# Two blocks of the last output, one early product, and rows of x turned a unit sooner

## The chip, the cores and the metric

The kernel runs on one core of a Trainium2 chip. A core has a matrix engine (TensorE, PE in the profile), a vector engine (VectorE, DVE), a scalar engine (ScalarE, ACT), GpSimd (POOL) and SyncE (SP), which in this kernel only issues DMAs. ACT and POOL issue DMAs too, each in order with its other work. All engines run their own instruction streams and wait for one another through semaphores. The metric is the device time of one execution in microseconds; three runs of the kernel before gave a median of 887.59 us (887.34 to 888.34).

## What is computed

Two blocks one after the other, in float32, for 4 sequences of 768 rows. The first is attention with 8 heads of 64 columns, in which a query sees only the keys that fall to the same of 16 centroids; the second is a normalization with a two-layer network and a residual.

```python
q_assign = argmax(q_n @ c_n.T); k_assign = argmax(k_n @ c_n.T)
scores = where(q_assign == k_assign, q @ k.T / sqrt(64), -1e9)
x = softmax(scores) @ v                      # (4, 768, 512) when the heads are put side by side
xn = (x - mean(x)) / sqrt(var(x) + 1e-6) * g_ln
out = x + relu(xn @ w_ch1) @ w_ch2           # w_ch1 (512, 2048), w_ch2 (2048, 512)
```

## The kernel before

**Attention.** The 32 heads are worked on as 16 pairs, numbered 0 to 15, one pair after another; pair 13, for instance, is the second of sequence 3. For each pair PE makes the masked scores (`scores`, L401), ACT the exponentials (L396), PE the weighted values (`weigh`, L413), and DVE adds the exponentials up over the keys (`add_up`, L431), of which there are two halves, g = 0 and 1. `finish` (L457) has four parts: the denominators and their way through DRAM (0, 1), the multiply of the numerators by the reciprocals on DVE with the store of the result, `xT_d`, by SP (2, L506 and L507), and, for the first two sequences, the rows of x (3). For pair 13 part 3 does nothing but forget the tile. In the last pair the sums of each half are five additions of 128x768 (L438).

**The network, with fewer products.** A matrix product of two by two blocks is made with seven products instead of eight (the parts 1, 2, 6, 5, 7, 4, 3 of `first_layer`, L897), and sums of blocks are made ahead by DVE (`x_sum`, `w1_sums`). The first layer runs over eight units, j = 0 to 7 (`first_units`, L1335), each with seven such products: part 1 starts a PSUM bank and ACT copies it out as `p1` (L881), then later parts add to the same bank. For sequence 0 the second layer does the same (`second_layer`, L990). For sequences 1 to 3 the second layer is a *deep layer* (`deep_layer`, L1224): each of the seven products, in the order 4, 7, 1, 6, 5, 2, 3, is itself made with seven (the steps (m, way), L1019 to L1029). The last steps are (3, 1), (3, 2), (2, 4), (2, 3), (3, 6), (3, 5), (3, 7), (3, 4), (3, 3). Each is eight matmul instructions of 128x192, for which `deep_product` (L1134) takes weights from a ring of ten buffers that SP fills (`ring_load`, L1080), and DVE or ACT then moves the bank to SBUF with sums (L1157 to L1180). Steps 1, 6, 7, 4 of one m add to one bank, so that (3, 4) can start only when DVE has read the bank after (3, 7), into `u`.

**Rows of x.** Sequences 2 and 3 need x by rows for their statistics, while attention left it by columns in `xT_d`. Eight blocks have to be turned: a load (`columns_load`, L530), a DVE transpose, and four stores (`rows_out`, L516). Five of them are turned during sequence 0's second layer. The other three are turned during sequence 1's first layer, at the ends of units (`unit_end`, L1440): loaded at the ends of units 0, 2 and 4, turned at the ends of 1, 3 and 5, and their stores issued by SP at the beginning of the next unit's end (`leave`, L1448). At the end of unit 6 come the statistics of the next sequence (L608, L611) and four ring loads. The tiles come from the tag `row` of two buffers, which the two rows of statistics use too.

**The end.** In sequence 3's deep layer the right half of the output comes in quarters of 192 rows and 128 columns, each after its last step: (3, 2), (3, 7), (3, 4) and (3, 3). `last_part` (L1237) has DVE transpose a quarter in blocks of 32x32 (L1247) and stores it with four DMAs of 24 KB in runs of 128 bytes (L1251), dealt to the queues of SP, ACT and POOL.

**What sets the order.** In most of the kernel the order of the instructions on PE, DVE, ACT and SP is that of the program text (`manual_schedule`). In sequence 0's second layer that holds for PE and DVE alone, and a planner places the DMAs of SP and ACT. SP holds a DMA until the buffer it writes is free, and what is behind it waits.

Of the kernel before, what the change touches and what calls it, by code (L numbers as in the profile page):

```python
# [23 lines left out]
def kernel(  # L24
# [701 lines left out]
    with tc.manual_schedule(engines=order | {mybir.EngineType.Pool}):  # L726
        def extras(n, at):
            for job in extra.pop((n, at), ()):
                job()

        def turn_pair(n):
            for side in (1, 0):
                prep_transpose(n, side)
                load(n + 1, "qk"[side])

        def weight(n, part):
            begun = convert.get((n - 1, 1)) if part == 0 and n - 1 in BEGIN else None
            m = convert.get((n, part))
            if begun is not None:
                weight_end(begun)  # L740
            if m is not None:
                split_weight(m)
                if (part, n in BEGIN) != (1, True):
                    weight_end(m)

        def weight_end(m):
            join_weight(m)
            load_weight(m + 2)

        for n in range(len(pairs)):  # L750
            nxt = n + 1 < len(pairs)
            own = range(2 * NT * n, 2 * NT * (n + 1))
            if n == 0:
                turn_pair(1)
            elif nxt:
                prep_route(n + 1)
            load(n + 1, "v")
            for i in own:
                if i >= AHEAD:
                    scores(i)  # L760
                if n == 0 and i + 1 == NT:
                    prep_sims(1)
                    prep_route(1)
            extras(n, "scores")
            if 1 < n and nxt:
                finish(n - 2, 1)
            if n and n + 2 < len(pairs):
                turn_pair(n + 2)
            if not nxt:
                finish(n - 1, 1)  # L770
            add_up(n, 0)
            extras(n, "sums")
            if not nxt:
                finish(n - 2, 2)
                finish(n - 2, 3)
            if n and nxt:
                finish(n - 1, 0)
            if nxt:
                for piece in pieces[:4]:
                    prep_mask(n + 1, *piece)  # L780
            add_up(n, 1)
            if n == 0:
                turn_pair(2)
            for i in own[:NT]:
                weigh(i)
            if nxt:
                for piece in pieces[4:]:
                    prep_mask(n + 1, *piece)
            weight(n, 0)
            if n > 1 and nxt:  # L790
                finish(n - 2, 2)
                finish(n - 2, 3)
            extras(n, "weigh")
            for i in own[NT:]:
                weigh(i)
            if n + 2 < len(pairs):
                prep_sims(n + 2)
            elif nxt:
                finish(n, 0)
            weight(n, 1)  # L800
            extras(n, "end")
            if n + 2 == len(pairs):
                finish(n - 1, 1)
            if not nxt:
                for part in (2, 3):
                    finish(n - 1, part)
# [327 lines left out]
    def deep_product(st, m, way):  # L1134
        p = st[m]
        if way == 1:
            p["x"] = ps("x_ps")
        if way == 2:
            p["y"] = ps("y_ps")
        if way == 5:  # L1140
            p["z"] = ps("z_ps")
        name = {2: "y", 5: "z", 3: "z"}.get(way, "x")
        bank = p[name][:, :QC]
        w, a = ring["at"].pop((m, way)), st["q", m][way]
        for c in range(NQH):
            nc.tensor.matmul(  # L1146
                bank, w[:, c, :], a[:, c],
                start=way in (1, 2, 5) and c == 0, stop=c == NQH - 1, skip_group_check=True,
            )

        def part(t, r, j):
            return None if t is None else t[:, j].rearrange("p (t a r) -> p t a r", a=2, r=Q)[:, :, r]

        def rows_of(t):
            return t.rearrange("p (t r) -> p t r", r=Q)

        def put_in(o, x, of=bank):  # L1157
            if x is None:
                nc.scalar.copy(o, rows_of(of))
            else:  # L1160
                nc.vector.tensor_tensor(o, rows_of(of), x, ALU.add)  # L1161

        def kept_sum(key, r, j):
            t = p[key] = rows_of(hid.tile([P, HC], F32, tag="p", name=key, bufs=5)[:, :QC])
            put_in(t, part(p["add"], r, j))

        if way == 1:
            kept_sum("p1", 0, 0)
        elif way == 2:
            put_in(part(p["to"], 0, 0), p["p1"])  # L1170
        elif way == 6:
            kept_sum("u2", 0, 1)
        elif way == 7:
            kept_sum("u3", 1, 1)
        elif way == 4:
            put_in(part(p["to"], 1, 0), part(p["add"], 1, 0))
        elif way == 3:
            put_in(part(p["to"], 0, 1), p["u2"])
        if way == 7:
            put_in(part(p["to"], 1, 1), p["u3"], p["z"][:, :QC])  # L1180

# [42 lines left out]
    def deep_layer(b, more, st):  # L1224
# [3 lines left out]
        def ahead_of(m):  # L1228
            p = st[m] = {}
            onto = {2: 1, 3: 5}.get(m)  # L1230
            p["add"] = done.get(onto)
            p["to"] = done[m] = done[onto] if onto else unit(f"m{m}")

        def sum_onto(i, j):
            nc.vector.tensor_tensor(done[i], done[i], done[j], ALU.add)

        def last_part(o, way):  # L1237

            part = {2: (0, 0), 7: (1, 1), 4: (1, 0), 3: (0, 1)}.get(way)
            if part is None:  # L1240
                return
            r, j = part
            queues = {
                7: (nc.sync, nc.scalar, nc.gpsimd, nc.sync), 4: (nc.scalar, nc.gpsimd, nc.sync, nc.scalar),
            }.get(way, (nc.sync, nc.scalar))
            y = unit("y_end")[:, 0, :QC]
            nc.vector.transpose(y, o[:, j].rearrange("p (t a r) -> p t a r", a=2, r=Q)[:, :, r])  # L1247
            to = out[b].rearrange("(a r t) m -> a (r t) m", r=Q, t=NT)[r]
            for i in range(P // Q):
                m = MH + j * P + i * Q  # L1250
                queues[i % len(queues)].dma_start(  # L1251
                    out=to[:, m : m + Q], in_=y[i * Q : (i + 1) * Q].rearrange("r (t f) -> r t f", f=Q)
                )
# [35 lines left out]
        if more:  # L1289
# [8 lines left out]
            jobs[2, 3] = [rest(0, 0, 2), lambda: rest_load(b, 1)]  # L1298
            jobs[3, 6] = [lambda: x_sum(b + 1, 1)]
            jobs[3, 5] = [lambda: w1_sums(b + 1, 0, (0, 1))]  # L1300
            jobs[3, 4] = [lambda: x_sum(b + 1, 2)]
            later(
                rest(1, 1, 7), out_of(1, 1, 7), out_of(0, 0, 2), None,
# [68 lines left out]
    with tc.manual_schedule(engines={mybir.EngineType.PE, mybir.EngineType.DVE}):  # L1372
# [6 lines left out]
        norm_load(1)  # L1379
        rows_load(1, 0)  # L1380

        def column():
            return early.tile([P, S], F32, tag="col", name="col", bufs=2)

# [10 lines left out]
        def do(f, *args):  # L1395
            return lambda: f(*args)
# [24 lines left out]
            (7, 2): [turn_columns, do(norm_apply, 1, 1, 0), w2_whole],  # L1421
            (4, 0): [do(norm_apply, 1, 1, 1), do(norm_apply, 1, 1, 2)],
            (4, 1): [turn_columns, do(norm_apply, 1, 1, 3)],
            (4, 2): [do(x_sum, 1, 1), do(x_sum, 1, 2)],
            (3, 0): [do(x_sum, 1, 3)],
            (3, 1): [do(x_sum, 1, 4), do(w1_sums, 1, 0)],
            (3, 2): [],
# [7 lines left out]
    with tc.manual_schedule(engines=order | {mybir.EngineType.SP}):  # L1435
# [4 lines left out]
        def unit_end(b, j):  # L1440
# [29 lines left out]
                norm_stat_rows(b + 1)  # L1470
            leave(4)
            if b == 1:
                def row():
                    return xpool.tile([P, S], F32, tag="row", name="col", bufs=2)

                if turning and j % 2:
                    columns_turn(row, lambda out, in_: leaving.append((out, in_)))
                elif asked and j % 2 == 0:
                    columns_load(row)
            if j > 4:  # L1480
                for _ in range(4):
# [3 lines left out]
        for b in range(1, B):  # L1485
            deep[b] = {}
            if b + 1 < B:
                rows_load(b + 1, 0)
            if b == 1:
                outer["t"] = w2_back(1)  # L1490
                first_units(b, 0)
            else:
                first_layer(b, 0, 1)
                first_layer(b, 0, 2)
                first_layer(b, 0, 6)
                relu(1)
                w1_sums(b, 0, (2, 3))
                x_sum(b, 3)
                first_layer(b, 0, 5)
                first_layer(b, 0, 7)  # L1500
                x_sum(b, 4)
                w1_sums(b, 1)
            unit_end(b, 0)
            for j in range(1, NFH):
                first_units(b, j)
                unit_end(b, j)
            relu(len(summed))
            inner_sums(deep[b], ORDER[0], cs=slice(NQH - 1, NQH))
            if b == 1:
                first.close()  # L1510
                units = pool("units", 1)
            deep_layer(b, b + 1 < B, deep[b])
# [232 lines left out]
```

## Time and profile before

| | us |
|---|---|
| median of three runs | 887.59 (887.34 to 888.34) |
| the profiled execution | 888.41 |
| its span, from the first instruction to the last | 886.6 |
| PE busy | 871.5 (98%) |
| DVE busy | 704.6 (79%) |
| ACT busy | 402.7 (45%) |
| granted clock of PE, mean | 0.997 |

The span is 1.8 us shorter than the execution that holds it. Busy times are sums over instructions of an engine, overlaps counted once. In the lines that follow, a timeline row gives the start in us, the time to the end of the last of its instructions in us, engine, source line, operation, the tiles out and in, and the count; in brackets stands the idle time of the engine before it and what ended it. A row of waits gives who waited for what, the total in us, how many times, and the longest. SPq and ACTq are the queues of SP and ACT, whose rows are the times that issuing took.

### The profile page before, as it was taken

To read this page: it belongs to the slowest core of one execution; us is meant where nothing else is said; L and a number is where in the kernel's file an instruction comes from. 1 tells how busy PE (TensorE), PEld (TensorE's weight loads), DVE (VectorE), ACT (ScalarE), POOL (GpSimd) and SP (SyncE) were. 2 spreads that over 40 slices of the span, in tenths; PEclk is the share of its full clock that TensorE was granted. 3 is DMA by queue.
4 is the path that set the end of the run, shared out by engine and by line. 5 is a ranking of instruction groups with operands and counts; after the bars stand their busy time and mean duration, and the time that the engine had idled before them with its cause. 6 is when DMAs were issued, how large, how long until landed. Compare 5 with 4: busy or idle time off the path is not lost.

```text
span 886.6 us, 13193 instructions
## 1 busy us (share of the span) xinstructions
PE 871.5 (98%) x4644; PEld 575.0 (65%) x4644; DVE 704.6 (79%) x1149; ACT 402.7 (45%) x739; POOL 77.8 (9%) x143
## 2 busy tenths in 40 slices
PE   8999999999999999999999999999999999999995
PEld 5444444444444445568885558996557997557995
DVE  6899999999999878959577787997556896646774
ACT  6777788888898823330004552103552101333110
POOL 1012121212222212110000000000000000000000
PEclk9999999999999999999999999999999999999998
DMA  7777899999886337876675878854236862511875
GB/s 159 134 131 129 150 173 186 209 203 190 184 197 172 97 117 202 235 197 215 186 175 183 261 239 293 299 155 98 57 71 204 284 190 54 110 62 37 275 201 98
DMA packets 251642, 151.01 MB, mean 170 GB/s; under 512 B 193696, under 2 KB 209200, under 8 KB 250544
## 3 DMA queue, kind: packets, MB, share of 16 engines
q1 hardware_dynamic: 219824, 130.75, 56.0%
q0 software_dynamic: 7776, 15.03, 8.7%
q10 hardware_dynamic: 23968, 4.30, 2.7%
q8 instruction: 39, 0.64, 0.3%
q14 instruction: 35, 0.29, 0.1%
HBM read 108.40 MB, written 33.25 MB: 160 GB/s over the span
## 4 chain that ended last, share of the span: by engine, by line
PE 93%; DMA 2%; DVE 2%; issue 1%; SPq 1%; ACT 1%; POOL 0%; DVEq 0%; ACTq 0%; POOLq 0%
PE x_ps L855 19%; PE s_ps L401 16%; PE a_ps L413 12%; PE x_ps L1146 12%; PE z_ps L855 9%; PE z_ps L1146 6%; PE x_ps L963 5%; PE y_ps L855 5%; PE y_ps L1146 3%; PE z_ps L963 2%; PE sim_ps L320 1%; PE den_ps L469 1%; PE y_ps L963 1%; DVE es L438 1%; DMA flat<-dsb 1%
## 5 line engine op out<-in xcount | busy, mean ns | idle before, releaser
L401 PE MATMUL s_ps<-t,t 64*128 64x384 f32 x768 | 154.8, 483 | 0.0
L401 PEld LDWEIGHTS s_ps<-t,t 64*128 64x128 f32 x768 | 67.9, 187 | 39.0 <-issue 38.3
L1146 PE MATMUL x_ps<-lower,w 128*128 128x192 f32 x448 | 81.0, 327 | 1.9 <-DMA w<-w_d 1.0
L886 DVE TENSOR_TENSOR lower<-z_ps,u 128x384 f32<-128x384 f32 x56 | 31.1, 555 | 60.1 <-PE z_ps L855 48.9
L1146 PEld LDWEIGHTS x_ps<-lower,w 128*128 128x128 f32 x448 | 74.0, 190 | 4.0 <-DVE u L1161 1.5
L396 ACT ACTIVATE e<-s_ps 128x768 f32<-128x768 f32 x84 | 67.1, 812 | 7.0 <-PE s_ps L401 6.4
L396 ACT ACTIVATE w<-s_ps 128x768 f32<-128x768 f32 x80 | 64.5, 813 | 8.3 <-PE s_ps L401 7.7
L401 PE MATMUL s_ps<-mask,mask 64*128 64x384 bf16 x384 | 62.7, 323 | 1.0 <-ACT e L396 0.6
L894 ACT ACTIVATE lower<-lower 128x384 f32<-128x384 f32 x88 | 45.0, 522 | 37.7 <-DVE lower L886 37.7
L881 ACT COPY u<-x_ps 128x384 f32<-128x384 f32 x64 | 30.7, 479 | 68.3 <-PE x_ps L855 68.3
L413 PE MATMUL a_ps<-e,v_sb 128*64 128x384 f32 x336 | 57.6, 488 | 0.0
L881 ACT COPY p<-x_ps 128x384 f32<-128x384 f32 x32 | 15.1, 471 | 91.4 <-PE x_ps L855 88.7
L413 PE MATMUL a_ps<-w,v_sb 128*64 128x384 f32 x320 | 55.2, 488 | 0.0
L855 PE MATMUL x_ps<-xt,ws 128*128 128x384 f32 x128 | 46.6, 487 | 0.9 <-ACT p L881 0.9
L855 PE MATMUL x_ps<-xn,ws 128*128 128x384 f32 x128 | 46.6, 487 | 0.0
L855 PE MATMUL x_ps<-xn,w 128*128 128x384 f32 x128 | 46.6, 487 | 0.0
L855 PE MATMUL z_ps<-xt,ws 128*128 128x384 f32 x128 | 46.5, 486 | 0.0
L855 PE MATMUL y_ps<-xn,w 128*128 128x384 f32 x128 | 46.5, 486 | 0.0
L855 PE MATMUL x_ps<-xt,w 128*128 128x384 f32 x128 | 46.5, 486 | 0.0
L855 PE MATMUL z_ps<-xn,ws 128*128 128x384 f32 x128 | 46.5, 486 | 0.0
L413 PEld LDWEIGHTS a_ps<-e,v_sb 128*64 128x64 f32 x336 | 23.5, 137 | 31.8 <-issue 28.7
L1251 POOL DMA_DIRECT2D out_dram<-y_end x2 | 1.2, 584 | 489.7 <-DMA out_dram<-y 488.6
(226 smaller groups left out, 1677.9 us busy)
## 6 DMA issues: line engine op xcount, KB each, us to landing
w<-w_d SPq DMA_DIRECT2D x84, 256.0 KB, 3.5
raw<-in_moe_w_ch_dram SPq DMA_DIRECT2D x32, 512.0 KB, 4.9
w<-w_t SPq DMA_DIRECT2D x36, 256.0 KB, 5.3
w<-tb POOLq DMA_DIRECT2D x32, 256.0 KB, 5.5
w_d<-wt SPq DMA_DIRECT2D x7, 1024.0 KB, 5.5
w<-w_all SPq DMA_DIRECT2D x27, 256.0 KB, 3.1
v_sb<-in_v_dram SPq DMA_DIRECT2D x32, 192.0 KB, 4.3
xr<-x_d SPq DMA_DIRECT2D x24, 256.0 KB, 2.8
```

The lines of the kernel that those rows point to most:

```text
L320: nc.tensor.matmul(sim[r : r + Q, :HC], cT[:, pr, :, :].rearrange("p j c -> p (j c)"), prepared[n][side][:, g * HC : (g + 1) * HC], start= ...
L396: nc.scalar.activation(e, s[:, :, :HC], AF.Exp, scale=SCALE)
L401: nc.tensor.matmul(s[:, j, :HC], of_keys[:, keys], of_queries[:, o : o + HC], start=part == first, stop=part != first, skip_group_check=True,)
L413: nc.tensor.matmul(acc[j * D : (j + 1) * D, :HC], loaded[n]["v"][:, j, c, :], e[:, j, :], start=(c == 0), stop=(c == NT - 1),)
L438: nc.vector.tensor_tensor(es, e[0] if m == 1 else es, e[m], ALU.add)
L469: nc.tensor.matmul(den[r : r + Q, :HC], ones, sums[n, g][h][:, j, :], start=h == 0, stop=h == parts - 1, tile_position=(0, r), skip_group_ ...
L855: nc.tensor.matmul(bank[:, :HC], lhs[:, c, :], rhs[:, c], start=first and c == 0, stop=c == NDH - 1, skip_group_check=True,)
L881: nc.scalar.copy(t, bank[:, :HC])
L886: nc.vector.tensor_tensor(h, bank[:, :HC], other, ALU.add)
L894: nc.scalar.activation(h, h, AF.Relu)
L963: nc.tensor.matmul(bank[:, :MH].rearrange("p (h f) -> p h f", h=2), hidden[lhs + (c,)][:, tt * P : (tt + 1) * P], rhs[:, :, c], start=firs ...
L1146: nc.tensor.matmul(bank, w[:, c, :], a[:, c], start=way in (1, 2, 5) and c == 0, stop=c == NQH - 1, skip_group_check=True,)
```

## The change

Four things are edited.

1. In the last pair of the attention, parts 2 and 3 of `finish` for pair 13 are called after `add_up(15, 1)` instead of before it.
2. In the deep layers of sequences 1 and 2, the first product of the next sequence's first layer is made after step (3, 7), in front of (3, 4); it no longer opens the next sequence.
3. The sixth block of x is loaded during sequence 0's second layer, after product (4, 2), and the three turns stand at the ends of units 0, 2 and 4 instead of 1, 3 and 5; the loads stand at the ends of 1 and 3.
4. The last two quarters of the output, (3, 4) and (3, 3), are summed into a tile of their own with the rows in order, turned by PE in two halves of 96 rows, copied out of PSUM by DVE and ACT, and stored with one DMA each by SP and ACT, in runs of 512 bytes. Of the quarter (3, 7), the fourth store goes to POOL instead of SP.

```diff
@@ in the loop over the pairs
             extras(n, "sums")
-            if not nxt:
-                finish(n - 2, 2)
-                finish(n - 2, 3)
...
             add_up(n, 1)
+            if not nxt:
+                finish(n - 2, 2)
+                finish(n - 2, 3)
@@ in deep_product
-        elif way == 4:
-            put_in(part(p["to"], 1, 0), part(p["add"], 1, 0))
-        elif way == 3:
-            put_in(part(p["to"], 0, 1), p["u2"])
+        elif way in (4, 3):
+            r, j = (1, 0) if way == 4 else (0, 1)
+            to = part(p["to"], r, j)
+            if "ends" in p:
+                p["ends"][way] = unit("end")[:, 0, :QC]
+                to = p["ends"][way].rearrange("p (r t) -> p t r", r=Q)
+            put_in(to, part(p["add"], 1, 0) if way == 4 else p["u2"])
@@ in deep_layer
+            if m == ORDER[-1] and not more:
+                p["ends"] = {}
...
-            queues = {
-                7: (nc.sync, nc.scalar, nc.gpsimd, nc.sync), 4: (nc.scalar, nc.gpsimd, nc.sync, nc.scalar),
-            }.get(way, (nc.sync, nc.scalar))
+            queues = (nc.sync, nc.scalar, nc.gpsimd, nc.gpsimd) if way == 7 else (nc.sync, nc.scalar)
+            if way in (4, 3):
+
+                columns = st[ORDER[-1]]["ends"][way]
+                turned, y = ps("turned"), unit("y_end")
+                n = QC // 2
+                for i in range(2):
+                    nc.tensor.transpose(
+                        turned[:n, i * P : (i + 1) * P], columns[:, i * n : (i + 1) * n], ident
+                    )
+                    copy = (nc.vector.tensor_copy, nc.scalar.copy)[i]
+                    copy(y[:n, i, :P], turned[:n, i * P : (i + 1) * P])
+                    (nc.sync, nc.scalar)[i].dma_start(
+                        out=out[b, r * QC + i * n : r * QC + (i + 1) * n, MH + j * P : MH + (j + 1) * P],
+                        in_=y[:n, i, :P],
+                    )
+                return
...
             jobs[3, 5] = [lambda: w1_sums(b + 1, 0, (0, 1))]
+            jobs[3, 7] = [lambda: first_layer(b + 1, 0, 1)]
             jobs[3, 4] = [lambda: x_sum(b + 1, 2)]
@@ in sequence 0's second layer
-            (4, 2): [do(x_sum, 1, 1), do(x_sum, 1, 2)],
+            (4, 2): [do(x_sum, 1, 1), do(x_sum, 1, 2), do(columns_load, row)],
@@ in unit_end
-                if turning and j % 2:
+                if turning and j % 2 == 0:
                     columns_turn(row, lambda out, in_: leaving.append((out, in_)))
-                elif asked and j % 2 == 0:
+                elif asked and j % 2:
                     columns_load(row)
@@ at the start of sequences 2 and 3
-                first_layer(b, 0, 1)
                 first_layer(b, 0, 2)
```

More of the change, by code (lines that the diff above doesn't have):

```diff
@@ L1380, with row @@
         rows_load(1, 0)
+        def row():
+            return xpool.tile([P, S], F32, tag="row", name="col", bufs=2)
         def column():
@@ L1472, in unit_end @@
             if b == 1:
-                def row():
-                    return xpool.tile([P, S], F32, tag="row", name="col", bufs=2)
-                if turning and j % 2:
+                if turning and j % 2 == 0:
                     columns_turn(row, lambda out, in_: leaving.append((out, in_)))
-                elif asked and j % 2 == 0:
+                elif asked and j % 2:
                     columns_load(row)
```

## The prediction

> **What bounds the kernel now.** I read the page, then TensorE's (PE's) waits, then the timelines around each wait and at the end.
>
> ```profile
> span 886.6 us, 13193 instructions
> ...
> PE 871.5 (98%) x4644; PEld 575.0 (65%) x4644; DVE 704.6 (79%) x1149; ACT 402.7 (45%) x739; POOL 77.8 (9%) x143
> ```
>
> PE is the bound: no edit here takes products away, so only what lies outside its 871.5 us can be won, 15.1 us in all. Its waits (total, times, longest) name places that the diff touches:
>
> ```profile
> PE x_ps L1146 <- DVE u L1161: 1.4, 3, 0.5
> ...
> PE x_ps L1146 <- DMA w<-w_d: 1.0, 1, 1.0
> PE x_ps L855 <- ACT p L881: 0.9, 1, 0.9
> ```
>
> The first is three stalls, one in each deep layer between products (3, 7) and (3, 4). The timeline of PE shows what such a stall costs:
>
> ```profile
> 599.65 1.46 PE L1146 MATMUL x_ps<-lower,w 128*128 128x192 f32 x8
> 601.57 1.57 PE L1146 MATMUL x_ps<-lower,w 128*128 128x192 f32 x8 [0.45 <-DVE u L1161]
> ```
>
> The gap is 0.45. In the chain of waits a product that follows another without a gap adds 1.30, but this one adds 1.57: a stall also costs a restart of 0.27, so 0.7 each.
>
> **A: the multiply of pair 13 behind the last key sums.** The stall at 322.65 waits for ACT's copy of `p`, and that for DVE's sums `es`, in order behind the multiply of L506:
>
> ```profile
> 317.14 0.95 DVE L645 TENSOR_TENSOR xn<-xn 128x768 f32<-128x768 f32 x1
> 318.01 0.95 DVE L506 TENSOR_TENSOR rb<-x,rb 128x768 f32<-128x768 f32 x1
> 318.88 0.95 DVE L438 TENSOR_TENSOR es<-e 128x768 f32<-128x768 f32 x1
> ```
>
> ```profile
> 322.11 0.48 ACT L881 COPY p<-x_ps 128x384 f32<-128x384 f32 x1 [2.64 <-DVE es L438]
> ```
>
> Moved, its slot (318.88 - 318.01 = 0.87) comes free: the copy ends at 321.72 instead of 322.59. The product before is done at 321.70, so a gap of about 0.07 and the restart stay. **Gain 0.87**; most, the gap, 0.94, with the restart, 0.27: 1.2. Least 0, if the copy meets another wait. What is late now: the multiply itself (to about 323.2) and its one 384 KB store on SP, from 318.99 to about 324.2, just ahead of pair 14's store at 324.98. Only a column load much later reads it. DVE's total up to 324.0 is the same, so pair 14's multiply and the first hidden sum behind it (324.87) do not move. From 322.7 to 543.8 PE is busy 221.1 of 221.1 us, with no other wait to swallow the gain.
>
> **B: one product of the next sequence between (3, 7) and (3, 4).** It happens twice (sequences 2 and 3). The product moved takes 1.29 (chain of waits); DVE's `u` is ready 0.45 after (3, 7) ends, so the product covers it. **Gain 2 x 0.7 = 1.4**; the third stall stays. The operands are there: its rows' last scaling is in step (5, 5), its set of sums in (3, 5). What becomes tight: the step's ACT copy of 0.48 is issued earlier on an ACT that had idled 18.6 us; the moved product no longer separates (3, 3) from the next two. The second sum of x, which product 6 needs, ended at 604.40 and product 6 began at 606.85; it now begins 0.7 sooner and the sum ends about 0.6 later (1.29 - 0.7), so 1.1 us of room is left. Product 7's sum (done 609.21, used 609.43) has only 0.2, but both ends hang on product 2's end, which moves with them. Bounds: 0 (another wait takes the place) to 1.42.
>
> **C: rows of x turned one unit sooner.** A turn is one DVE transpose (0.94 to 0.98) and, a unit later, four stores of 96 KB on SP; its load is one 384 KB DMA on SP. Of the three turns left, the last one's stores now stand in front of the statistics and the next weights:
>
> ```profile
> 526.30 6.50 SPq L1216 DMA_DIRECT2D x_d<-col  x4
> 532.90 1.58 SPq L1064 DMA_DIRECT2D w_d<-wt  x1
> 534.58 0.46 SPq L608 DMA_DIRECT2D stat_d<-st  x1
> 538.94 0.86 SPq L611 DMA_DIRECT2D stat_row<-stat_d  x2
> 539.85 0.42 SPq L1088 DMA_DIRECT2D w<-w_d  x1
> ```
>
> ```profile
> 544.84 2.84 PE L1146 MATMUL x_ps<-lower,w 128*128 128x192 f32 x16 [0.99 <-DMA w<-w_d]
> ```
>
> PE's weights issued at 539.85 landed after 4.86 (chain of waits), 0.99 late. With the stores a unit earlier (about 513 to 520, where SP waited 8.4 for DVE), `w_d` goes when DVE's last difference is done, at 532.34 or up to 0.94 sooner. I keep 4.36 from the statistics' store to the load and 0.91 from there to the weights, and take 0.37 (its usual issue) for 1.58: weights at 532.4 + 0.4 + 4.36 + 0.9 = 538.1 at the latest, 1.75 sooner where 0.99 is needed. **Gain 0.99 + 0.24** (2.84 against 2 x 1.30) **= 1.23**; least 0, if the landing is slower by more than 0.76. The costs: 0.97 of DVE in the first unit, which was busy 6.62 of 9.10 us there; the w1 sums behind it would end at 482.6, and the product that reads them starts at 485.5, so it hides. The other turns move into units with 6.8 and 6.5 of about 9. On SP the stores now precede that unit's weight stores; their readers follow two units later.
>
> **D: the tail.** Before, the last two quarters go through a DVE transpose (0.38), then four stores each:
>
> ```profile
> 878.31 0.38 DVE L1247 STREAM_TRANSPOSE y_end<-m 128x192 f32<-128x192 f32 x1
> ```
>
> ```profile
> 879.97 1.25 ACTq L1251 DMA_DIRECT2D out_dram<-y_end  x2
> 880.42 0.57 SPq L1251 DMA_DIRECT2D out_dram<-y_end  x1
> ```
>
> The data are ready at 878.69, but the queues are not: SP's last issue ends at 880.99 and ACT's at 881.22, and the span 5.4 later. One issue of the quarter before took 1.66 on SP. The change removes two transposes and eight stores; it adds four transposes on PE, two copies on DVE, two on ACT and four stores, so that SP issues 3 instead of 5, ACT 3 instead of 5, POOL 2 as before, its second 1.0 earlier (0.58 to issue, 3.7 to land: over by 881).
> Against it, PE must wait for DVE's sum of (3, 4) before it transposes, and product (3, 3) is queued behind: 0.36 + two hops of 0.04 + restart 0.27 + two transposes of 0.11 (128 columns where 192 take 1.30/8; the first ones in the kernel took 0.21) = 0.95. The last product ends at 877.89 + 0.95 = 878.84, its sum at 879.23, the transposes at about 879.6 and 879.75 (272 ns for one with 128 columns), ACT's copy (0.25 for 128 columns at L607) at 880.05, its issue (0.32 to 0.58) at 880.4 to 880.65, 0.57 to 0.82 sooner; SP's, by the DVE copy (0.3, below the 0.36 of 192 columns), at about 880.4, 0.6 sooner. **Gain 0.55**, a little under both, as the two new sums write with a stride that no row shows: each takes 0.36 if it is free, as it is for the strides of L1161, and 0.72 if it doubles them, which would cost 0.72 on the path. Bounds: a gain of 0.9, and a loss of 0.95 if the queues take as long behind the last product as now.
> The row here says that what counts is the issues, not the transpose. The Trainium skill ("VectorE: DVE Perf Modes", section "The three transpose paths") speaks against the edit: it gives 311 ns on VectorE and 390 ns on TensorE for 128x128 in bf16. By that alone the two quarters would lose 0.16 us and the forecast would be 884.2.
>
> **Sum.** 0.87 + 1.4 + 1.23 + 0.55 = 4.05. The profiled execution took 888.41 (span 886.6 and 1.8 around it) and would take 884.4; it lay 0.8 above the median of 887.59, against which the forecast is **883.5**. The bounds together: 1.2 + 1.42 + 1.23 + 0.9 = 4.75 gives 882.8; the forecast's own range is 882.8 to 884.6.
>
> **Rivals.**
> 1. The tail loses: PE's wait of 0.95 is paid and the queues give nothing back. For: one cross-engine wait is added in front of the last product. Against: four stores fewer to issue. 883.5 + 0.55 + 0.95 = 885.0. Chance 0.15.
> 2. A or C does not do what it says: another wait takes its place. For: C depends on a landing of 4.86 that the same bytes may stretch. 884.4 or 884.7, both 885.6. Chance 0.12.
> 3. SP blocks in sequence 0's second layer: the order of SP's queue there is the planner's, and the moved load's buffer is free only when DVE's subtractions with the first row end at 449.14. If it lands ahead of the second row's load (second issue of 439.0), that goes 10 us late, and the scaling at 450.75 waits until 449.2 + 5.4 = 454.6, or 3.8: 887.3, no change. Against: SP already waits up to 8.6 for DVE in that layer, and PE does not stall in it. Chance 0.11, all mishaps that end within 0.2% included.
> 4. Slower: the granted clock falls because PE has fewer breaks. Each 0.1% of it costs 0.87 us; from 0.46% it eats the gain, from 0.67% it is slower; at 0.990 instead of 0.997, 883.5 + 6.1 = 889.6. Against: from 322.7 to 543.8 without a break the clock is 1.00. Chance 0.07.
>
> **How the numbers follow.** The forecast has 0.55. A measurement of this kernel tells some 0.2% (1.8 us) from no change: faster below 885.8, slower above 889.4. Faster: 0.55 + 0.15 + 0.12 = 0.82; same 0.11; slower 0.07. The range takes in the first three, 882.8 to 885.6.
>
> **What would show it.** A: at 322 no wait of `x_ps` for `p` over 0.1. B: the waits for `u` once instead of three times. C: no wait for `w_d`, the four `x_d` stores before 521 and the weights before 539. D: a new wait of about 0.9 in front of the last product, and the last issue at 880.4 less the 3.5 won earlier. I am wrong if new waits of PE stand between 545 and 875, or if the distance from PE's last product to the span's end (8.7) shrinks by less than 0.95.

## The result and the profile after

The changed kernel took a median of 885.88 us in 18 runs: 17 took 884.54 to 887.96, and one, in a slow state with a granted clock of 0.947, took 919.96 and is left out of the ratio. The kernel before, beside it, took 887.61 (886.94 to 888.34, 18 runs). That is a ratio of 0.998, 95% interval 0.9972 to 0.9987, or 1.7 us faster with 1.15 to 2.5 as its bounds. The direction was right; the time forecast, 883.5 within 882.8 to 885.6, was not: less than half of the 4.05 us came. The profiled execution took 885.48 us, 2.9 less than the one before.

The page's head:

```profile
span 883.7 us, 13207 instructions
...
PE 871.6 (99%) x4648; PEld 574.7 (65%) x4648; DVE 704.5 (80%) x1149; ACT 402.8 (46%) x741; POOL 78.3 (9%) x143
```

PE does as much as before, so all that was won lies in its gaps. Its waits (total, times, longest):

```profile
PE turned L1255 <- DVE end L1161: 1.2, 2, 0.6
PE y_ps L1146 <- ACT lower L894: 1.1, 1, 1.1
...
PE turned L1255 <- DVE y_end L1259: 0.8, 2, 0.4
...
PE x_ps L1146 <- DVE u L1161: 0.4, 1, 0.4
```

The waits for `p` and for `w_d` are gone, and that for `u` comes once instead of three times, as forecast. But a wait of 1.1 for ACT's `lower` is new, and the transposes wait four times. The timeline of PE at A, at C and at B, in order of time:

```profile
320.43 0.48 ACT L881 COPY p<-x_ps 128x384 f32<-128x384 f32 x1 [1.47 <-DVE es L438]
...
321.02 1.50 PE L855 MATMUL x_ps<-xt,ws 128*128 128x384 f32 x4
```

```profile
538.50 0.52 ACT L894 ACTIVATE lower<-lower 128x384 f32<-128x384 f32 x1 [3.25 <-DVE lower L886]
...
539.08 0.59 PE L1146 MATMUL y_ps<-lower,w 128*128 128x192 f32 x2 [1.13 <-ACT lower L894]
...
543.65 2.76 PE L1146 MATMUL x_ps<-lower,w 128*128 128x192 f32 x16
```

```profile
599.61 1.45 PE L855 MATMUL x_ps<-xn,w 128*128 128x384 f32 x4
599.81 0.36 DVE L1161 TENSOR_TENSOR u<-x_ps,m 128x192 f32<-128x192 f32 x1 [0.58 <-PE x_ps L1146]
...
600.90 1.46 PE L1146 MATMUL x_ps<-lower,w 128*128 128x192 f32 x8
```

At A, `p` is out at 320.91 and the product starts without a wait. At B the moved product covers `u`, whose sum ends at 600.17. At C the weights no longer hold PE at 543.65, but 4.6 us ahead of them it has stood for 1.13: product (4, 2) of the deep layer needs the relu of the first layer's last unit, which ended at 539.02.

How far PE is ahead of the kernel before, instruction by instruction, gives each part its share:

| between | forecast | traces |
|---|---|---|
| the start to 322 us, ahead of all four edits | 0 | 0.5 |
| A | 0.87 | 1.1 |
| C | 1.23 | -0.4 |
| B, up to the end of product (3, 4) of sequence 3 | 1.4 | 1.6 |
| D, up to the span's end | 0.55 | 0.1 |
| sum | 4.05 | 2.9, or 2.4 without the start |

The 0.5 of the start belongs to no edit. In the 14 profiled executions of this study the 1700th matmul, ahead of every edit, starts between 243.1 and 244.4; before and after, shown here, have 243.7 and 243.2.

**Where C went.** DVE's waits from 465 to 545 us, sequence 1's first layer:

```profile
DVE col L518 <- DMA col<-xT_d: 6.1, 2, 3.2
DVE wt L1063 <- DMA w_t<-w_t: 2.6, 1, 2.6
DVE lower L886 <- ACT u L881: 2.3, 1, 2.3
```

Before, DVE never waited there for `col`, and 1.3 for `w_t`:

```profile
529.72 0.69 DVE L1063 TENSOR_TENSOR wt<-w_t 128x512 f32<-128x512 f32 x1 [1.31 <-DMA w_t<-w_t]
```

SP's queue after the change says why:

```profile
500.92 2.47 SPq L1219 DMA_DIRECT2D x_d<-col  x4
503.49 0.60 SPq L1064 DMA_DIRECT2D w_d<-wt  x1
504.13 0.65 SPq L1042 DMA_DIRECT2D w_t<-w_t  x1
504.83 1.33 SPq L534 DMA_DIRECT2D col<-xT_d  x1
...
515.01 2.13 SPq L1219 DMA_DIRECT2D x_d<-col  x4
521.91 0.38 SPq L1064 DMA_DIRECT2D w_d<-wt  x1
522.33 0.50 SPq L1042 DMA_DIRECT2D w_t<-w_t  x1
```

The last block's load goes out at 504.83, behind four stores of 96 KB, a store of weights and a load of weights, of 1 MB each. It takes 9 us to land, where the median of the loads of x whose landing is on record is 3.9 (longest 9.3 in this kernel, the second block's, issued at 486.46; 6.2 before). The same queue of the kernel before shows what was different:

```profile
496.87 0.72 SPq L534 DMA_DIRECT2D col<-xT_d  x1
...
503.92 0.50 SPq L1042 DMA_DIRECT2D w_t<-w_t  x1
504.51 6.92 SPq L1216 DMA_DIRECT2D x_d<-col  x4
512.53 0.38 SPq L1064 DMA_DIRECT2D w_d<-wt  x1
512.96 0.50 SPq L534 DMA_DIRECT2D col<-xT_d  x1
521.93 0.37 SPq L1064 DMA_DIRECT2D w_d<-wt  x1
```

The load of `w_t` stands at the ends of the odd units (503.92, and 486.15 and 522.34), the loads of x stood at those of the even ones, right behind a store of weights but not behind a load of them. The change put them at the odd ends, behind `w_t`. The load at 496.87 had four stores of x and 1 MB of weights' store ahead of it too, and took the 6.2; the changed kernel adds the 1 MB of `w_t`. From 505.5 to 513.9 the DMA engines are busy to 99% and move 352 GB/s, at which 1 MB takes 3.0 us: an estimate that would explain the step from 6.2 to 9, though no run moved `w_t` by itself. What the late landing holds up is written in DVE's row:

```profile
514.01 0.98 DVE L518 STREAM_TRANSPOSE col<-col 128x768 f32<-128x768 f32 x1 [3.19 <-DMA col<-xT_d]
...
521.80 0.95 DVE L1106 TENSOR_TENSOR w<-fifth,lower 128x768 f32<-128x768 f32 x1
...
529.91 0.69 DVE L1063 TENSOR_TENSOR wt<-w_t 128x512 f32<-128x512 f32 x1 [2.62 <-DMA w_t<-w_t]
```

DVE runs in program order, so 3.19 of waiting stand in front of all its later work of the layer. (The second block's load made it wait 2.94, up to 495.95, but that it made good in time in which it had stood idle before: it is through with unit 4's differences of weights at 510.81, before at 512.50.) The difference behind which SP issues `w_d` and `w_t` comes at the same clock time as before (`w_t` at 522.33, before 522.34), although PE is 1.6 ahead. So `w_t` lands late for DVE (2.62), its last sums end late, the relu too, and PE stands at (4, 2).

**Where D went.** The end of the timeline:

```profile
872.22 1.57 PE L1146 MATMUL x_ps<-lower,w 128*128 128x192 f32 x8 [0.45 <-DVE u L1161]
...
873.83 0.50 DVE L1161 TENSOR_TENSOR end<-x_ps,m 128x192 f32<-128x192 f32 x1 [0.86 <-PE x_ps L1146]
...
874.38 0.31 PE L1255 MATMUL turned<-ident,end 128*96 128x128 f32 x1 [0.59 <-DVE end L1161]
874.73 0.29 DVE L1259 COPY y_end<-turned 96x128 f32<-96x128 f32 x1 [0.41 <-PE turned L1255]
...
875.08 0.31 PE L1255 MATMUL turned<-ident,end 128*96 128x128 f32 x1 [0.38 <-DVE y_end L1259]
...
875.23 1.47 PE L1146 MATMUL z_ps<-lower,w 128*128 128x192 f32 x8
...
877.98 0.32 PE L1255 MATMUL turned<-ident,end 128*96 128x128 f32 x1 [0.38 <-DVE y_end L1259]
878.33 0.26 ACT L1259 COPY y_end<-turned 96x128 f32<-96x128 f32 x1 [2.64 <-PE turned L1255]
878.62 0.33 ACTq L1260 DMA_DIRECT2D out_dram<-y_end  x1
```

Rows of products that follow each other without a wait overlap by 0.16. So (3, 3) could have started 0.16 before the end of (3, 4)'s row, at 873.63 (this is what "the end of (3, 4)" means from here on); it starts at 875.23, 1.6 later, not 0.95: the sum into the strided tile takes 0.50, not 0.36, and the second half's transpose waits until DVE has copied the first half out of the same PSUM tile. The last issue ends 5.3 after the end of (3, 4). Before, it was 4.8 in this execution.

### The profile page after: what moved, and what is told of

The parts are those of the page before. It is cut to its first block, busy times and chain, and to the rows that moved or that the text cites. A ratio compares the mean times of both kernels' runs of the same rounds, so it can differ in the third digit from the quotient of the medians.

```text
span 883.7 us, 13207 instructions
## 1 busy us (share of the span) xinstructions
PE 871.6 (99%) x4648; PEld 574.7 (65%) x4648; DVE 704.5 (80%) x1149; ACT 402.8 (46%) x741; POOL 78.3 (9%) x143
## 4 chain that ended last, share of the span: by engine, by line
PE 97%; DVE 1%; DMA 1%; ACT 0%; issue 0%; ACTq 0%
PE x_ps L855 18%; PE s_ps L401 18%; PE a_ps L413 14%; PE x_ps L1146 12%; PE z_ps L855 9%; PE z_ps L1146 6%; PE x_ps L963 5%; PE y_ps L855 5%; PE y_ps L1146 3%; PE z_ps L963 2%; PE sim_ps L320 1%; PE den_ps L469 1%; PE y_ps L963 1%; DMA k_sb<-in_k_dram 0%; DMA q_sb<-in_q_dram 0%; ACT lower L894 0%
```

## The experiments

In most of them theory 1 is the reading above, theory 2 the forecast's own terms, with the loss only where they meet, and theory 3 or a rival has the gain taken by something else; each expectation says what its theories are. For the tail, "the queues set the end" stood against "PE sets it". The times are medians, each beside runs of the kernel before on the same chip.

### Each part alone

A alone: only the move of `finish(n - 2, 2)` and `(n - 2, 3)`.

```diff
             add_up(n, 1)
+            if not nxt:
+                finish(n - 2, 2)
+                finish(n - 2, 3)
```

> The kernel before with part A alone (pair 13's multiply behind the last key sums). Theory 1, read from the two traces (PE's place gains 1.11 us at the stall near 322, and nothing takes it back): 1.1 us faster, 886.5. Theory 2, the forecast's terms, with the loss in their combination: 0.87 faster, 886.7. Theory 3 (a gain in the attention is swallowed by the weight loads near 538, which do not move with PE): the stall near 322 is gone, the one near 543 grows, and the time is 887.3 or more.

B alone:

```diff
+            jobs[3, 7] = [lambda: first_layer(b + 1, 0, 1)]
...
-                first_layer(b, 0, 1)
```

> The kernel before with part B alone (one product of the next sequence between (3, 7) and (3, 4)). Theories 1 and 2: two of three stalls of 0.45 with their restarts are gone, 1.4 us faster, 886.2. If the next sequence's start gives it back: 887.6, with a new wait of PE between 605 and 615.

C alone:

```diff
-            (4, 2): [do(x_sum, 1, 1), do(x_sum, 1, 2)],
+            (4, 2): [do(x_sum, 1, 1), do(x_sum, 1, 2), do(columns_load, row)],
...
-                if turning and j % 2:
+                if turning and j % 2 == 0:
...
-                elif asked and j % 2 == 0:
+                elif asked and j % 2:
```

> The kernel before with part C alone (rows of x turned one unit sooner). Theory 1: the turn in unit 4 waits some 3 us for its load, DVE's chain up to the relu in front of (4, 2) stays where it was in absolute time, so the wait for w_d (0.99 and its restart) goes and a wait for that relu of 0.3 to 0.9 comes: 0.3 to 0.7 faster, 887.1. Theory 2: 1.23 faster, 886.4, no new wait. Theory 3, that C costs in itself as in the trace after (0.43): 888.0.

D alone: the edits in `deep_product`, `ahead_of` and `last_part`.

```diff
+            if way in (4, 3):
...
+                    nc.tensor.transpose(
+                        turned[:n, i * P : (i + 1) * P], columns[:, i * n : (i + 1) * n], ident
+                    )
```

> The kernel before with part D alone (two quarters turned by PE). Theory 1: PE's stall in front of (3, 3) is 1.6 us, not 0.95, and the last issue comes only as much sooner as the span after showed: 0.1 to 0.2 faster, 887.45, no difference. Theory 2: 0.55 faster, 887.05.

Eleven runs of each, beside 888.82 for the kernel before (886.48 to 890.88, 33 runs):

| | median us | ratio, 95% interval |
|---|---|---|
| A | 887.53 (886.15 to 889.02) | 0.9986 (0.9977 to 0.9995) |
| B | 886.95 (885.97 to 888.57) | 0.9979 (0.9970 to 0.9988) |
| C | 888.86 (887.89 to 891.43) | 1.0002 (0.9992 to 1.0012) |
| D | 888.61 (887.11 to 889.37) | 0.9999 (0.9990 to 1.0008) |

A and B give about what was forecast, C and D nothing that can be told. C's interval allows a gain of 0.7 at most, so C misses its 1.23 by itself, not in how the parts meet. D's allows 0.9, which still holds the 0.55: this run does not settle D. A is not swallowed by the weights near 543, as theory 3 had it: PE's wait for `w_d` stays at 1.0. With C alone the new wait of PE is there, without the other edits:

```profile
PE y_ps L1146 <- ACT lower L894: 1.2, 1, 1.2
```

### All but C

C undone, the other three kept.

```diff
-            (4, 2): [do(x_sum, 1, 1), do(x_sum, 1, 2), do(columns_load, row)],
+            (4, 2): [do(x_sum, 1, 1), do(x_sum, 1, 2)],
...
-                if turning and j % 2 == 0:
+                if turning and j % 2:
...
-                elif asked and j % 2:
+                elif asked and j % 2 == 0:
```

> The changed kernel with part C undone (the three turns at the ends of units 1, 3, 5 again). Theory 1 (C gives back what A won, as DVE waits for the third turn's load): 2.5 to 3 us faster than before if the wait for w_d stays at 0.99, but that wait grows as PE now comes 1.1 us sooner to weights that come when they came: 2.0 to 2.6 faster, 885.3, no slower than the changed kernel. Theory 2 (C gains 1.23 and D loses): slower than the changed kernel by about 1.2, 887.1.

885.65 us (885.14 to 886.24) beside 888.60: 0.9964 (0.9952 to 0.9976). PE's waits have `w_d` back, here 1.4 long, and none for `lower`:

```profile
PE x_ps L1146 <- DMA w<-w_d: 1.4, 1, 1.4
```

A, B and D without C gain as much as with it, or more: 0.9964 against 0.998 and, run again, 0.9972. Theory 2, a loss of 1.2 against the changed kernel, falls; the gain of 3.0 by the medians is a little over theory 1's 2.0 to 2.6.

### The two loads issued behind their turns

All four edits, but the second and third loads go out as soon as a turn has been given to DVE, at the ends of units 0 and 2, instead of a unit later.

```diff
                 if turning and j % 2 == 0:
                     columns_turn(row, lambda out, in_: leaving.append((out, in_)))
-                elif asked and j % 2:
                     columns_load(row)
```

> The changed kernel, with the loads of the second and third turn issued directly behind the turns of units 0 and 2, a unit sooner. Theory 1 (the third turn's load, which stood behind that unit's stores and 2 MB of weights and landed 9 us after its issue, holds DVE for 3.2 us): no wait of the turn for its load, w_t asked for about 1.7 us sooner, the wait of (4, 2) for its relu under 0.3, and 0.8 to 1.3 us faster than the changed kernel, 884.7. Rival (DVE's chain is bound by the landing of w_t, 7.5 us whatever asks for it): the wait for the load goes, the wait for w_t grows by as much, the time is that of the changed kernel, 885.9.

884.64 us (883.71 to 885.06) beside 888.60: 0.9954 (0.9940 to 0.9967). No load of x whose landing is on record takes longer than 4.9, DVE does not wait for `col`, and PE has no wait at all between 30 and 870 us. DVE's waits from 465 to 545 us, and then SP's queue:

```profile
DVE wt L1063 <- DMA w_t<-w_t: 1.5, 1, 1.5
```

```profile
520.87 0.45 SPq L1042 DMA_DIRECT2D w_t<-w_t  x1
...
536.45 0.38 SPq L1088 DMA_DIRECT2D w<-w_d  x1
```

`w_t` goes out 1.5 sooner than in the changed kernel, as far as PE is ahead, and C wins 1.15 in PE's place (from 1.55 ahead to 2.70), or 1.23 with the restart behind it (2.78), the forecast's 1.23. In the four other kernels with the early loads below, the 1.15 comes as 1.0 to 1.2. That is the proof for the loads: the turns, the stores and the weights stand where the change put them, and only two loads moved, out from behind `w_t`. The time says so too: on the same chip the kernel without C took 885.65, and the runs of the two do not overlap (at most 885.06 here, at least 885.14 there).

### Each half in its own PSUM tile

The changed kernel, with the two halves of a quarter turned into two PSUM tiles.

```diff
-                turned, y = ps("turned"), unit("y_end")
+                y = unit("y_end")
...
-                for i in range(2):
+                turns = [ps("turned") for _ in range(2)]
+                for i, turned in enumerate(turns):
```

> The changed kernel, with each half of a turned quarter in a PSUM tile of its own. Theory 1 (the second transpose waits for DVE's copy of the first out of the same tile, 0.38 and its restart, twice): both waits gone, the stall in front of (3, 3) 1.0 instead of 1.6, the last issue about 1.0 sooner: 0.8 to 1.1 us faster than the changed kernel, 885.0. Rival (the end is set by something else, such as the branch behind the last instruction or the landing of the stores): no change, 885.9.

885.75 us (884.75 to 886.90) beside 888.60: 0.9967 (0.9955 to 0.9979). The stall before (3, 3) falls from 1.60 to 1.01, and the end from 10.1 to 9.7 behind the end of (3, 4). One of the two waits for a copy went, that of (3, 4); before the second transpose of (3, 3) it stays, so that the last issue comes 0.6 sooner and not the 1.0 of theory 1. In time it is not told apart from the changed kernel.

Both mends together, the early loads and the two tiles:

> The changed kernel with both edits, the sooner loads and the two PSUM tiles. Theory 1: the two gains add up, 1.6 to 2.4 us faster than the changed kernel, 883.9. Rival: as many of them as failed alone are missing.

883.92 us (883.26 to 884.34) beside 888.60: 0.9945 (0.9932 to 0.9959), theory 1's 883.9. Its end (the timeline of PE) has the two transposes of (3, 4) back to back, but those of (3, 3) still one behind the other's copy. All four tiles come from one PSUM pool of two buffers, and where only (3, 3) is turned, as in a kernel below, its two are back to back; that the reuse of the buffers is the cause is not shown.

```profile
873.45 0.42 PE L1256 MATMUL turned<-ident,end 128*96 128x128 f32 x2 [0.59 <-DVE end L1161]
...
876.47 0.31 PE L1256 MATMUL turned<-ident,end 128*96 128x128 f32 x1 [0.38 <-DVE y_end L1260]
```

### The changed kernel again, and the tail taken apart

These four ran on one chip, beside 888.68 (887.42 to 889.94, 13 runs). The first is the changed kernel, unedited.

> The changed kernel itself, beside the three that follow. Both theories: 1.7 us less than the kernel before (ratio 0.998), PE's new wait of 1.1 before product (4, 2) there again, the stall before the last product 1.6.

886.53 us (885.39 to 887.03): 0.9972 (0.9962 to 0.9982). In this profiled execution the late load was worse, and C cost PE 1.8 where the first execution lost 0.4, C alone 0.5 and the kernel with two tiles 0.7. The row of DVE's waits:

```profile
DVE col L518 <- DMA col<-xT_d: 7.5, 2, 4.3
```

The last load took 9.8 to land. In these four executions with late loads, all eight landings of the second and third load are 9.0 to 9.8. C's price varies more than the landing does.

The second has the early loads and the old tail (the edits of D taken out):

```diff
-        elif way in (4, 3):
+        elif way == 4:
+            put_in(part(p["to"], 1, 0), part(p["add"], 1, 0))
+        elif way == 3:
+            put_in(part(p["to"], 0, 1), p["u2"])
```

> A, B and C with the two loads issued behind their turns; the tail as it was before. Theory 'the tail brings next to nothing' (0.14 in the trace): within 0.5 us of the same kernel with the tail (884.64 against a kernel before of 888.6, a gain of 4.0), so a gain of 3.5 to 4.0. Rival, the forecast's own 0.55 or more: a gain of 3.4 or less. Rival, the tail loses: a gain of over 4.2. In the trace the distance from the end of product (3, 4) to the span's end should be 10.2 to 10.7, as in the kernels before without the tail.

884.72 us (884.27 to 886.17): 0.9960 (0.9947 to 0.9974), by the ratio a gain of 3.6. The same kernel with the tail had 0.9954. The difference, 0.5 us in favour of the tail, is smaller than either interval, so the time decides between 0.14 and 0.55 for D no more than the first runs did. The distance from the end of (3, 4) to the span's end is 10.65, within the 10.2 to 10.7 expected. Over all profiled executions it was 10.22, 10.21, 10.73, 11.34 and 10.65 with the old tail, on average 10.6, and 10.08, 10.21, 10.55, 10.40 and 10.19 with the changed tail, on average 10.3. That is 0.3 in favour of D, less than the 1.1 by which the old tail varies: a hint, no proof.

The third has the early loads, two tiles, and only the last quarter turned by PE; (3, 4) goes through DVE and four stores as before.

```diff
-            if "ends" in p:
+            if "ends" in p and way == 3:
...
-            if way in (4, 3):
+            if way == 3:
```

> Loads early, and only quarter (3, 3) turned by PE, each half in its own PSUM tile; quarter (3, 4) by DVE's transpose and four stores as before, in the old order of queues. Theory 'the stall of PE in front of (3, 3) eats the gain': without it (1.0 to 1.6 us) the last product ends that much sooner; but SP and ACT have one store more each (0.6), so the end is 0 to 0.5 us sooner than with both quarters in two tiles (gain 4.7): a gain of 4.7 to 5.2. Rival 'the queues set the end': the four stores of (3, 4), 1.25 us of two queues or so, are back, and the gain falls to 4.2 or less.

883.25 us (882.49 to 884.42): 0.9945 (0.9931 to 0.9959), 4.9 us by the ratio and 5.4 by the medians. It has the shortest profiled span of all:

```profile
span 880.9 us, 13203 instructions
```

```profile
872.08 1.46 PE L1146 MATMUL z_ps<-lower,w 128*128 128x192 f32 x8
...
873.58 0.50 DVE L1161 TENSOR_TENSOR end<-z_ps,u 128x192 f32<-128x192 f32 x1 [0.53 <-PE z_ps L1146]
...
874.13 0.42 PE L1258 MATMUL turned<-ident,end 128*96 128x128 f32 x2 [0.59 <-DVE end L1161]
...
874.62 0.26 ACT L1262 COPY y_end<-turned 96x128 f32<-96x128 f32 x1 [17.04 <-DMA out_dram<-y_end]
...
874.91 0.35 ACTq L1263 DMA_DIRECT2D out_dram<-y_end  x1
```

PE goes from (3, 4) into (3, 3) without a stall. The last issue ends 3.2 behind the end of (3, 4), where the changed kernel has 5.3, the two tiles 4.7 and the kernels with the old tail 4.8 to 6.2. The span ends 8.8 behind it, against 10.1 to 10.6, 9.6 to 9.9, and 10.2 to 11.3. So in the trace the stall did eat D's gain. The time itself is at the theory's 4.7 to 5.2, but its interval does not exclude the rival's 4.2, and by the ratio it equals both quarters in two tiles (0.9945). Against the changed kernel of the same four the intervals do not touch, but the early loads have a part in that.

The fourth has the early loads, two tiles for both quarters, and eight matrix multiplications on PE behind the last transposes, whose result is used by nothing. Each is two instructions in the trace, 16 in all, as the four of a product are its eight.

```diff
+                if way == 3:
+                    idle = ps("idle")
+                    for c in range(8):
+                        nc.tensor.matmul(idle[:, :QC], ident, columns, start=c == 0, stop=c == 7, ...)
```

> Loads early, two tiles, and 8 more matrix multiplications of 128x192 (1.3 us) on PE behind its last transposes, which nobody reads. Theory 'with the tail, PE, that has work up to the end, closes the program last': the span behind the last transpose grows by about 1.3, a gain of about 3.4 in place of 4.7. Rival 'the last stores set the end, as before': nothing changes, a gain of 4.7.

883.54 us (883.12 to 884.09): 0.9944 (0.9931 to 0.9958), what the same kernel had without them (0.9945).

```profile
span 882.3 us, 13239 instructions
```

```profile
876.59 2.77 PE L1268 MATMUL idle<-end,ident 128*128 128x192 f32 x16
...
877.08 0.33 ACTq L1261 DMA_DIRECT2D out_dram<-y_end  x1
```

PE worked 2.6 us longer, to 879.4 (it took twice the 1.3 that I had reckoned), and the span is no longer than the 882.6 without it. My theory that PE closes the program last falls. It rested on PE's last steps in the changed trace coming late, which they do without deciding anything. The rival stands: what counts is the last stores. In the nine executions in which PE turns (3, 3), the landing of the last issued store is on record, and in each the span ends 1.8 to 1.9 behind it; with the old tail the last landings are on record only in part.

This kernel also says what D is worth with two tiles. Beside the early loads with the old tail, on the same chip, it is 1.2 faster, and the five runs of the one do not overlap with those of the other (at most 884.09 here, at least 884.27 there).

## Why the prediction was right or wrong

**A was right, and a little low.** It measured 1.1 us in the trace and 0.4 to 2.0 alone by its interval. "A gap of about 0.07 and the restart stay" did not hold: `p` came 1.7 sooner (320.91 against 322.59), 0.5 of that from the start, and the whole stall went, as the part's upper bound of 1.2 had it.

**B was right.** It holds twice, with 1.6 in the trace for 1.4. Of what it made tight, nothing turned into a wait.

**C failed, and it is the larger part of the error: 1.6 us.** The step that failed is "The costs", which went through DVE's time, the stores and the weights, and left out the loads that move with the turns. The prediction did say when the weights would go out ("538.1 at the latest"; they went at 537.95) and that their wait would be gone, and both hold. But of the three loads, only the first was followed, in rival 3. From the last load's issue to the place of its turn there are 6.0 us after the change (504.83 to 510.81, where DVE came free); before, it had 9.9 (512.96 to 522.86), and landings of up to 6.2. Of this the trace of before showed a part: the new place of the load, behind `w_t` (504.42), and the new place of the turn (512.50) lie 8.1 apart in it, and `w_t` itself takes 7.4 to land there. That little room could have been seen; the 9 us could not be read off any row. Rival 2 had the outcome right in kind ("another wait takes its place"), with the wrong landing.

**D was mis-sized: 0.1 in one pair of executions, 0.3 on average, for 0.55, neither clear of what executions differ by.** The view of the end was right in that the stores set it and PE does not, as the extra work on PE and the constant distance behind the last landing show. What failed is the sum of 0.95 for PE's stall (its terms, as written, add up to 0.93), which measured 1.60. It took the two transposes as one piece; the copy between them, and the restart after it, are the most of the difference (with two tiles the stall is 1.01), and the strided sum the rest (0.50 for the 0.36 taken; the 0.72 of a doubling did not come). The same copy comes again behind the last product, so that the last issue ended 2.25 after that product instead of 1.56 to 1.81. The kernel in which only the last quarter is turned has 1.7 there, from 873.54 to 875.26, as reckoned. The sign that was to prove D right, a distance from the last product to the span's end that shrinks by 0.95, came (8.7 to 7.0), and PE's stall of 1.6 took it back. A sign that counts only one side of a trade proves nothing. The other sign, new waits of PE between 545 and 875, looked past the place: C's new wait ended at 539.08.

The page that I weighed against D, the Trainium skill, "VectorE: DVE Perf Modes", section "The three transpose paths", has TensorE's path as the longer one, for 128x128 in bf16. The runs, in float32 with 128x192, agree in sign and go further: from the sum's end to the last half in SBUF it takes 1.36 with one PSUM tile and 0.80 with two, where DVE's transpose of the quarter took 0.38.

With C and D as they measured, and A and B too, the forecast's sum is 2.4 and the time 885.2, 0.7 below the median of 885.88. The rest is within what C varies by: it cost 0.4 to 1.8 in the four profiled executions with late loads.

The rivals: SP did not block in sequence 0's second layer, and the clock was 0.997 to 0.999 in the 17 runs, against 0.997 in the profiled execution before, so 3 and 4 fall. Rivals 1 and 2 each hold in part, together, which the range's upper end did not reckon with: 883.5 with C's 1.23 and D's 0.55 both at nothing is 885.3, and the stretch that C lost on top is the rest.

What stays open: why the last store, the second half by ACT, takes 3.3 us to land in the changed kernel, from 878.62 to 881.94, when SP's store of the first half, issued 0.67 sooner, takes 1.5; what the 1.8 us behind that landing are, which close the span; and the value of D with one tile, since the distance it changes varies by 0.5 to 1.1 between executions of the same tail.

## What to carry to other kernels

When a step is moved, follow each of its transfers to the engine that waits for it: write down the distance from issue to use, before and after, and compare it with the longest landing on that queue, not the median, and with the bytes that will be queued ahead of it. Here a load was better issued behind the instruction that frees its buffer than a unit later, behind that unit's stores and weights. Work given to the bounding engine in front of its last product is paid in full, with every copy between its pieces; behind it, PE's own time was free here, and only the chain to the last store counted.

## What the runs showed of the hardware

- A DVE sum of 128x192 in float32 takes 0.50 when it writes with a stride of six elements, and 0.36 with runs of 32.
- Two PE transposes of 128x96 in float32, back to back, take 0.42, and DVE's transpose of the 128x192, in blocks of 32x32, 0.38. Where both wrote one PSUM tile, the second waited 0.38 for the copy of the first.
- One load of 384 KB took 3.1 to 9.8 us to land: 4.9 behind a store of 1 MB on its queue, 5.4 to 6.2 in sequence 1's first layer in the kernels without C, and 9.0 to 9.8 behind 384 KB of stores and the weights' store and load of 1 MB each, with the DMA engines busy to 99%.
- 2.6 us of PE's work behind its last transpose cost nothing; the span ended 1.8 to 1.9 behind the landing of the last store in the nine executions in which PE turns (3, 3).
- The first 243 us, in which nothing differs, ended within a range of 1.3 us over 14 executions, as much as several of the effects looked for here.
